# Early operands for the first backward steps of an attention and FFN gradient, and unread TensorE products while its opening waits

## The chip, the cores and the metric

One core of one Trainium2 chip runs the whole program. The metric is the device time of one execution in microseconds (us), of which each kernel was run several times; profiles are of one execution each.

Engine names in the profiles: PE is TensorE's products, PEld its weight loads, DVE VectorE, ACT ScalarE, POOL GpSimd, SP SyncE, whose queue (SPq) issues most transfers (900 of 1066 issues in the trace of the kernel before).

## The reference, cut to what matters

The reference is a transformer block, forward and backward: x of 2048 rows by 448, 16 heads of 28, an FFN of width 1792, in bf16. Outputs are the block's result and the six gradients.

```python
xn = _layernorm(x)
return x + _A_ref(xn, wqkv, wo) + _B_ref(xn, w_gate, w_up, w_down)
# _A_ref: softmax attention, 16 heads;  _B_ref: (silu(x @ w_gate) * (x @ w_up)) @ w_down
_out, _vjp = jax.vjp(_f, A_x, A_wqkv, A_wo, B_w_gate, B_w_up, B_w_down)
return (_out, *_vjp(grad_out))
```

## The kernel before

The kernel runs one fixed order of instructions. An **opening** normalises x, transposes it and makes the first projections. The **forward half** is 256 slots of attention (one key tile, four heads), with the FFN's forward and backward products and most weight gradients filled in between. The **backward half** is 512 steps: `row(k)` computes a score product and a dP product for two heads, `ew(k)` the exponentials (ACT) and ds = dP * e (DVE), and later products use them. Between the halves is the **turn**: the last forward buffers are free only now, and the buffers of the backward half are opened in their place.

`sp_flush()` issues stores that were put off.

```python
def turn_loads():
    nonlocal kq
    sp_flush()                      # four stores of dw_oT are still held here
    ffst.close()
    kq = bwd.enter_context(tc.tile_pool(name="kq", bufs=1, side="right", reuse_waits="tile"))
    SP.dma_start(out=new_k(0, 0)[:], in_=KD_d[0, 0])
    for qc in range(4):
        SP.dma_start(out=new_q(0, qc)[:], in_=QD_d[0, qc])
    SP.dma_start(out=new_k(0, 1)[:], in_=KD_d[0, 1])
```

After the last slot come six last units (PV product, normalisation, output gradient, the softmax correction `mid3`, the projection gradient `dwo_unit`), and the first four backward rows stand between the pieces of the last five:

```python
for u in last[:-5]:
    run(u())
k = n = 0
for u in last[-5:]:
    for _ in u():
        n += 1
        if n in (8, 17, 25, 32):
            row(k)
            ew(k)
            k += 1
K0 = k
sp_flush()                          # stores of odT, the transpose that mid3 issued
fwd.close()
...
for x in pend:                      # DMA transposes of the first ds tiles
    x()
fT = bk.tile([P, 4, 2, 4, P], BF16, name="dsp", bufs=1)
drip(("f",), [(fT[:, a:a + 2], fT_d[:, a:a + 2]) for a in (0, 2)], 10)

def late_dw(c):                     # the last FFN weight gradients, from step 9
    have(("f",))
    ps = ps_g.tile([P, 2, P], FP32, name="genb")
    for t in range(NT):
        PE.matmul(ps[:dn], lhsT=xn_sp[:, t, d0:d0 + dn], rhs=fT[:, t // 4, :, t % 4, :], ...)
```

`late_dw`: its operand `fT` (tile `dsp` in the trace) is stored to HBM at the forward end and loaded back behind the transposes.

The opening, cut:

```python
for t in range(4):
    run(T_unit(xnT, xn_t, t, t % 2 == 0, ps_s if t < 2 else None))   # transposes of x
...
proj(1, 0, True)                    # key, then query projection of the first 512 rows
proj(0, 0)
for c in range(3):
    slot(4 * c); ...
    T(t + 2, t + 3)
    proj(1, c + 1)
```

The softmax here doesn't subtract the row's maximum and nothing guards it: scores larger than these inputs give would overflow.

## Time and profile before

| kernel before, profiled execution | us |
|---|---|
| median of 3 executions (range) | 1441.15 (1439.99 to 1442.68) |
| first exponentials of the forward half | 15.9 |
| exponentials of the last forward slot, 255 | 606.5 |
| first product of backward step 0 | 614.1 |
| first gradient accumulation | 623.0 |
| exponentials of backward step 48 | 689.0 |

Two more views of the kernel before matter in hindsight. The first is the order of time of SP's queue around the turn (start, time of the issue, queue, line, kind, out<-in, count). It was not in the prediction, and most of this document hangs on it:

```profile
607.22 2.12 SPq L206 DMA_DIRECT2D out_dram<-dw_oT  x4
...
619.96 1.29 SPq L200 DMA_TRANSPOSE odT<-od  x1
...
623.67 4.26 SPq L829 DMA_TRANSPOSE dsT<-ds_sb  x3
627.99 1.08 SPq L769 DMA_DIRECT2D dsp<-fT_d  x2
```

Read it as a chain: four stores, then (in the prediction) the loads of keys and queries, then the transpose of od, then three transposes of ds, then the load of dsp. Each stands behind the one ahead of it in one queue. In the kernel before nobody waits for the last one, because TensorE itself comes late.

The second is the granted clock between two stretches of 3.4 us (columns as in the prediction):

```profile
621.30:624.70 3.40, 1.65 (x15) 0.40 (x12) 2.46 (x5) 1.05 (x3) 1.48 (x3) 1.00 0.70 192
624.80:628.20 3.40, 3.40 (x26) 0.61 (x26) 2.85 (x5) 2.14 (x6) 0.53 (x2) 0.50 1.00 189
```

TensorE was busy for 1.65 of 3.40 us and was then given half clock for the next 3.4 us. The stretch behind that, 628.20 to 631.60 us with TensorE busy for 2.58 of 3.40 us, was at full clock and was followed by half clock as well (0.50 from 631.60 to 635.00).

### The profile page before, as it was taken

The numbers are of one execution on the slowest core, as the hardware profiler recorded it, in microseconds if no ns is written. First come the engines' busy times: TensorE is split into PE (matmuls) and PEld (weight loads), VectorE is DVE, ScalarE is ACT, GpSimd is POOL, SyncE is SP. The second block draws the span as 40 slices with busy tenths as digits, with TensorE's granted clock in tenths as the row PEclk, the third lists the DMA queues.
The fourth block names the chain that finished last, engine by engine and source line by source line (L and its number), as shares of the span: only waits on it lengthen the run. The fifth ranks groups of instructions, "written<-read, shape, count | busy, mean of one in ns | idle before, by whom it ended". The sixth has DMA issues, their size and how long they took to land. (4 is left out here: it accounts for less than half of the span.)

```text
span 1440.1 us, 34682 instructions
## 1 busy us (share of the span) xinstructions
PE 1326.3 (92%) x12647; PEld 541.0 (38%) x12708; DVE 1151.8 (80%) x1997; ACT 1261.5 (88%) x2193; POOL 403.6 (28%) x561
## 2 busy tenths in 40 slices
PE   5889999999999999889999999999999999999996
PEld 2333333333333333333333434433443444444343
DVE  6667757666676676578998998888889999989988
ACT  5789988988889999869989989899989999989974
POOL 6464524464334454111112112201111011010006
PEclk9999999999999999989999999999999999999998
DMA  5796956796678586799999999999999999999971
GB/s 154 181 199 165 235 122 160 187 195 164 146 162 192 147 172 145 178 234 226 226 213 217 232 220 188 196 209 229 228 173 194 209 223 230 201 191 203 198 142 60
DMA packets 681179, 271.69 MB, mean 189 GB/s; under 512 B 606424, under 2 KB 655824, under 8 KB 681008
## 3 DMA queue, kind: packets, MB, share of 16 engines
q1 hardware_dynamic: 672576, 255.35, 87.1%
q0 software_dynamic: 7024, 13.82, 4.1%
q8 instruction: 100, 1.64, 0.5%
q14 instruction: 71, 0.58, 0.1%
q10 hardware_dynamic: 1408, 0.30, 0.1%
HBM read 65.09 MB, written 60.36 MB: 87 GB/s over the span
## 5 line engine op out<-in xcount | busy, mean ns | idle before, releaser
L842 DVE TENSOR_TENSOR ds_sb<-db,e_sb 128x512 bf16<-128x512 f32 x1024 | 646.8, 684 | 51.3 <-issue 21.1
L836 ACT ACTIVATE e_sb<-sb 128x512 bf16<-128x512 f32 x1024 | 554.8, 611 | 60.4 <-PE db L820 44.5
L612 ACT ACTIVATE eT<-s_w 128x1024 bf16<-128x1024 f32 x256 | 263.5, 1029 | 46.1 <-PE s_ps L609 43.1
L614 ACT ACTIVATE eT<-s_ps 128x512 bf16<-128x512 f32 x512 | 280.4, 612 | 0.0
L820 PE MATMUL db<-kd,qd 32*128 32x512 bf16 x1024 | 234.4, 384 | 8.2 <-DVE ds_sb L842 7.4
L812 PE MATMUL sb<-kd,qd 32*128 32x512 bf16 x1024 | 210.4, 387 | 5.1 <-DMA qd<-QD_d 3.3
L961 POOL TENSOR_TENSOR dq_acc<-dq_acc,dq_st 128x256 f32<-128x256 f32 x64 | 46.2, 721 | 455.4 <-ACT dq_st L959 455.4
L919 PE MATMUL acc<-ds_sb,qd 128*32 128x512 bf16 x1024 | 161.0, 391 | 0.0
L915 PE MATMUL acc<-e_sb,qd 128*32 128x512 bf16 x1024 | 158.8, 391 | 1.3 <-DVE dw_o L528 1.3
L902 ACT COPY dsT<-db 128x1024 bf16<-128x1024 bf16 x128 | 130.1, 1016 | 14.6 <-PE db L897 13.9
L380 POOL TENSOR_TENSOR nn<-nn,ag 128x512 f32<-128x512 f32 x56 | 71.2, 1271 | 252.2 <-DVE ag L378 243.7
L609 PE MATMUL s_ps<-QQ,KK 32*128 32x512 bf16 x512 | 125.4, 385 | 3.9
L1128 PE MATMUL genb<-wguT,dau_c 128*128 128x448 bf16 x448 | 117.5, 355 | 6.3 <-ACT dq_st L959 3.9
L609 PE MATMUL s_w<-QQ,KK 32*128 32x512 bf16 x512 | 100.3, 387 | 13.1 <-ACT eT L612 10.4
L812 PEld LDWEIGHTS <-qd 32*128 32x128 bf16 x1024 | 48.2, 91 | 149.4 <-issue 140.3
L421 PE MATMUL gen<-xn_t,f_sp 128*128 128x448 bf16 x416 | 91.8, 354 | 2.6 <-DVE nn L395 1.7
L421 PEld LDWEIGHTS <-f_sp 128*128 128x128 bf16 x640 | 55.7, 98 | 75.0 <-issue 31.9
L946 PE MATMUL genb<-dsT,kd 128*32 128x256 bf16 x2048 | 79.5, 275 | 1.9 <-DVE dqT L955 0.6
L897 PE MATMUL db<-ident_bf,ds_sb 128*128 128x128 bf16 x1032 | 79.4, 220 | 1.1 <-DVE ds_sb L842 1.1
L897 PEld LDWEIGHTS <-ds_sb 128*128 128x128 bf16 x1032 | 68.3, 99 | 24.1 <-issue 5.3
L451 PE MATMUL gen<-eT,VS 128*32 128x512 bf16 x1024 | 68.4, 384 | 5.5 <-DVE nn L395 3.3
L381 POOL TENSOR_TENSOR nn<-nn,tt 128x512 f32<-128x512 f32 x56 | 72.0, 1286 | 4.4
(167 smaller groups left out, 1911.0 us busy)
## 6 DMA issues: line engine op xcount, KB each, us to landing
F_d<-hda SPq DMA_DIRECT2D x56, 384.0 KB, 3.1
dau_c<-F_d SPq DMA_DIRECT2D x24, 512.0 KB, 4.4
qd<-QD_d SPq DMA_DIRECT2D x16, 512.0 KB
kd<-KD_d SPq DMA_DIRECT2D x16, 384.0 KB, 4.0
dsT<-ds_sb SPq DMA_TRANSPOSE x383, 4.3
dc<-dqkvT_d SPq DMA_DIRECT2D x12, 384.0 KB, 3.9
h_c<-F_d SPq DMA_DIRECT2D x8, 512.0 KB, 4.4
wT_d<-wT_f SPq DMA_DIRECT2D x14, 256.0 KB, 3.6
```

What stands on the lines that cost most here:

```text
L421: PE.matmul(ps[:, :D], lhsT=fsp[fc][:, t // 4, w, t % 4, :], rhs=rhs[:, t, :], start=(t == 0), stop=(t == NT - 1))
L609: PE.matmul(sp4[hh], lhsT=KK[g][r:r + HP, kt * P:(kt + 1) * P], rhs=QQ[g][r:r + HP, qsl], start=True, stop=True, tile_position=(r, 0))
L612: ACTE.activation(out=e2[0][:], in_=wide[:], func=ACT.Exp, scale=SCALE)
L614: ACTE.activation(out=e2[1][:, j], in_=sp4[2 + j], func=ACT.Exp, scale=SCALE)
L812: PE.matmul(s_ps[:], lhsT=qside[g, qc][r:r + HP, 0, qi * P:(qi + 1) * P], rhs=kside[g, kc][r:r + HP, 0, :], start=True, stop=True, tile_po ...
L820: PE.matmul(d_ps[:], lhsT=qside[g, qc][r:r + HP, 1, qi * P:(qi + 1) * P], rhs=kside[g, kc][r:r + HP, 1, :], start=True, stop=True, tile_po ...
L836: ACTE.activation(out=est[k][:, j], in_=sps.pop((k, j))[:], func=ACT.Exp, scale=SCALE)
L842: DVE.tensor_tensor(out=ds[:, j], in0=dps.pop((k - 1, j))[:], in1=est[k - 1][:, j], op=ALU.mult)
L897: PE.transpose(ps[:, c, :], ds[:, c // 4, (c % 4) * P:(c % 4 + 1) * P], ident_bf[:])
L902: ACTE.copy(out=o, in_=ps[:])
L915: PE.matmul(a[r:r + HP, :], lhsT=sp4[:, 1, r:r + HP], rhs=e[:, j, :], start=first, stop=last, tile_position=(0, r), skip_group_check=True)
L919: PE.matmul(a[r:r + HP, :], lhsT=sp4[:, 0, r:r + HP], rhs=ds[:, j, :], start=first, stop=last, tile_position=(0, r), skip_group_check=True)
```

## The change

Its intent: take the wait for keys and queries out of the turn by loading the first operands 16 slots earlier into a free buffer, start the backward rows sooner, take work off DVE there, and keep TensorE's clock up in the opening with products that nobody reads. The diff, cut to its core:

```diff
+    def warm(ps, n):
+        for _ in range(n):
+            PE.matmul(ps[:], lhsT=ident_bf[:], rhs=ident_bf[:].unsqueeze(1).to_broadcast([P, 4, P]), start=True, stop=True)
 ...
+    warm(genx.tile([P, 512], FP32, name="gen"), 24)          # before the first transposes
-        proj(1, c + 1)
+        proj(1, c + 1, pre=3)                                # three before each of three projections
 ...
     for i in range(16, NS):
         slot(i)
+        if i == NS - 16:
+            sp_flush()
+            first4 = wk.tile([P, S], BF16, name="qk_sp", bufs=1)[:].rearrange("p (a s) -> p a s", a=4)
+            SP.dma_start(out=first4[:, 0:2], in_=KD_d[0, 0, :, 0:2])
+            SP.dma_start(out=first4[:, 2:4], in_=QD_d[0, 0, :, 0:2])
 ...                                                          # in row(k):
+            ks, qs = (first4[:, 0], first4[:, 2]) if k < 4 else (kside[g, kc][:, 0], qside[g, qc][:, 0])
 ...                                                          # in mid3, last call only:
+        (ACTE.copy if end else DVE.tensor_copy)(out=dOl, in_=prod[:])
+        (POOL if end else DVE).tensor_tensor(out=prod[:], in0=prod[:], ...)
+        eng = POOL if (g, qc) == (G - 1, 3) else DVE         # its four small operations
 ...                                                          # in dwo_unit, last call only:
+        (ACTE.copy if g == G - 1 else DVE.tensor_copy)(out=o[:], in_=ps[:, :D])
 ...
-    for u in last[:-5]:
+    for u in last[:-6]:
         run(u())
-    k = n = 0
-    for u in last[-5:]:
+    K0 = 5
+    row(0)
+    ew(0)
+    k = 1
+    for u in last[-6:]:
-            if n in (8, 17, 25, 32):
+            if n in (4, 20, 24, 32):
```

More of the change, by code (lines that the diff above doesn't have):

```diff
@@ L267, in qkv_open, with qkv_unit @@
         VS[g] = wk.tile([P, NT, P], BF16, name="VS")
-    def qkv_unit(g, tq, sc, act=False):
+    def warm(ps, n):
+        for _ in range(n):
+            PE.matmul(ps[:], lhsT=ident_bf[:], rhs=ident_bf[:].unsqueeze(1).to_broadcast([P, 4, P]), start=True, stop=True)
+    def qkv_unit(g, tq, sc, act=False, pre=0):
         if g not in QQ:
@@ L274, in qkv_unit @@
         ps = new_gen([P, 512], FP32, name="gen")
+        warm(ps, pre)
         for c in range(4):
@@ L503, in mid3 @@
         dl = wk.tile([P, 3, 16], FP32, name="dl")
-        DVE.tensor_copy(out=dOl, in_=prod[:])
-        DVE.tensor_tensor(out=prod[:], in0=prod[:], in1=t[:, 0].rearrange("p q (h r) -> p (q h) r", r=HP), op=ALU.mult)
+        end = (g, qc) == (G - 1, 3)
+        (ACTE.copy if end else DVE.tensor_copy)(out=dOl, in_=prod[:])
+        (POOL if end else DVE).tensor_tensor(out=prod[:], in0=prod[:], in1=t[:, 0].rearrange("p q (h r) -> p (q h) r", r=HP), op=ALU.mult)
         yield 0
@@ L508, in mid3 @@
         yield 0
-        DVE.tensor_scalar(out=dl[:, 1, :], in0=dl[:, 0, :], scalar1=-1.0, scalar2=None, op0=ALU.mult)
-        DVE.tensor_copy(out=dOl[:, :, 28], in_=dl[:, 1, :])
-        DVE.tensor_tensor(out=dl[:, 2, :], in0=dl[:, 1, :], in1=dOl[:, :, 28], op=ALU.subtract)
-        DVE.tensor_copy(out=dOl[:, :, 29], in_=dl[:, 2, :])
+        eng = POOL if (g, qc) == (G - 1, 3) else DVE
+        eng.tensor_scalar(out=dl[:, 1, :], in0=dl[:, 0, :], scalar1=-1.0, scalar2=None, op0=ALU.mult)
+        eng.tensor_copy(out=dOl[:, :, 28], in_=dl[:, 1, :])
+        eng.tensor_tensor(out=dl[:, 2, :], in0=dl[:, 1, :], in1=dOl[:, :, 28], op=ALU.subtract)
+        eng.tensor_copy(out=dOl[:, :, 29], in_=dl[:, 2, :])
         tT = wk.tile([P, 2, 4, P], BF16, name="odT")
@@ L527, in dwo_unit @@
         o = wk.tile([P, D], BF16, name="dw_o", bufs=1)
-        DVE.tensor_copy(out=o[:], in_=ps[:, :D])
+        (ACTE.copy if g == G - 1 else DVE.tensor_copy)(out=o[:], in_=ps[:, :D])
         for hh in range(4):
@@ L632, in T, with proj @@
             run(T_unit(xnT, xn_t, t))
-    def proj(tq, sc, act=False):
-        run(qkv_unit(0, tq, sc, act))
+    def proj(tq, sc, act=False, pre=0):
+        run(qkv_unit(0, tq, sc, act, pre))
     def stats4(cc):
@@ L811, in row @@
                 r = HP * (2 * hp + j)
-                PE.matmul(s_ps[:], lhsT=qside[g, qc][r:r + HP, 0, qi * P:(qi + 1) * P],
-                          rhs=kside[g, kc][r:r + HP, 0, :], start=True, stop=True, tile_position=(r, 0))
+                PE.matmul(s_ps[:], lhsT=qs[r:r + HP, qi * P:(qi + 1) * P],
+                          rhs=ks[r:r + HP], start=True, stop=True, tile_position=(r, 0))
                 sps[k, j] = s_ps
@@ L816, in row @@
             g, hp, kc, qc, qi = steps[k - 1]
+            ks, qs = (first4[:, 1], first4[:, 3]) if k <= 4 else (kside[g, kc][:, 1], qside[g, qc][:, 1])
             for j in range(2):
@@ L819, in row @@
                 r = HP * pv(2 * hp + j)
-                PE.matmul(d_ps[:], lhsT=qside[g, qc][r:r + HP, 1, qi * P:(qi + 1) * P],
-                          rhs=kside[g, kc][r:r + HP, 1, :], start=True, stop=True, tile_position=(r, 0))
+                PE.matmul(d_ps[:], lhsT=qs[r:r + HP, qi * P:(qi + 1) * P],
+                          rhs=ks[r:r + HP], start=True, stop=True, tile_position=(r, 0))
                 dps[k - 1, j] = d_ps
@@ L854 @@
     fill.mine = None
-    for u in last[:-5]:
+    for u in last[:-6]:
         run(u())
-    k = n = 0
-    for u in last[-5:]:
+    n = 0
+    K0 = 5
[3 more added lines that the diff above has]
+    for u in last[-6:]:
         for _ in u():
             n += 1
-            if n in (8, 17, 25, 32):
+            if n in (4, 20, 24, 32):
                 row(k)
@@ L864 @@
                 k += 1
-    K0 = k
     sp_flush()
```

## The prediction

> **What bounds the kernel now.** I read the page first, for which engine is full; then the table of busy time by stretch, for where it is not; then the order of time around the two places that the change edits, for what each wait ends on.
>
> The page's busy times and the two rows of slices:
>
> ```profile
> PE 1326.3 (92%) x12647; PEld 541.0 (38%) x12708; DVE 1151.8 (80%) x1997; ACT 1261.5 (88%) x2193; POOL 403.6 (28%) x561
> ...
> PE   5889999999999999889999999999999999999996
> ...
> PEclk9999999999999999989999999999999999999998
> ```
>
> TensorE is busy 90% or more nearly everywhere except in slices 1 to 3 (the opening), slices 18 and 19 (the turn from the forward to the backward half, near 610 us) and the end. In the forward half PE is busy 8.4 to 10 us of each 10 us, ACT 8 to 9.9; in the backward half PE 46 to 49 of each 50 us, with DVE and ACT close behind. So time saved at the two seams should reach the end: both halves are a static order of instructions on a nearly full engine. 512 backward steps in about 777 us are 1.52 us a step, and nothing there waits for a fixed hour.
>
> The turn, in stretches of 2 us (columns: stretch, length, busy time and count of PE, PEld, DVE, ACT, POOL, then granted clock, DMA share, GB/s):
>
> ```profile
> 608.00:610.00 2.00, 1.02 (x4) 0.36 (x4) 0.69 (x1) 0.52 (x2) 0.00 (x0) 1.00 0.48 109
> 610.00:612.00 2.00, 0.84 (x12) 0.65 (x10) 0.95 (x2) 0.00 (x0) 0.00 (x0) 1.00 0.71 191
> 612.00:614.00 2.00, 0.00 (x0) 0.00 (x0) 0.00 (x0) 0.00 (x0) 0.00 (x0) 1.00 1.01 403
> 614.00:616.00 2.00, 1.90 (x15) 1.04 (x16) 0.57 (x1) 1.12 (x3) 0.00 (x0) 0.63 0.98 350
> 616.00:618.00 2.00, 2.00 (x6) 0.60 (x4) 1.93 (x5) 1.05 (x2) 0.00 (x0) 0.51 1.05 420
> ```
>
> No engine works between 612 and 614 us while the DMA moves 403 GB/s, and then the granted clock is half. The order of time names the cause:
>
> ```profile
> 609.44 0.53 SPq L722 DMA_DIRECT2D kd<-KD_d  x1
> ...
> 610.23 0.61 PE L487 MATMUL gen<-woT,dyT 128*128 128x128 bf16 x8
> ...
> 614.10 0.39 PE L812 MATMUL sb<-kd,qd 32*128 32x512 bf16 x2 [3.27 <-DMA qd<-QD_d]
> ...
> 622.98 0.39 PE L915 MATMUL acc<-e_sb,qd 128*32 128x512 bf16 x2 [1.28 <-DVE dw_o L528]
> ```
>
> The first backward score product waits 3.27 us for kd and qd, whose issue (609.44) comes after the last forward buffers are free. From the last forward PV product (ends 608.94) to the first gradient accumulation (622.98) is 14.0 us. The work in it is far less: on PE, by durations and spacings at full clock, transposes 0.6, 16 products of the output gradient about 1.0, four rows about 1.8, 16 products of the projection gradient about 3.0: 6.4 us. On DVE: oacc 0.69, rl and od 0.95, prod 0.69, the last softmax correction 0.43 + 0.69 + 0.61 + 0.75 = 2.48, three pairs of ds products 3.9, dw_o 0.62: 9.3 us.
>
> The opening:
>
> ```profile
> 9.35 1.03 PE L320 MATMUL s_ps<-ident_bf,xn_t 128*128 128x128 bf16 x8 [9.35 <-DMA KK<-in_A_wo_dram]
> ...
> 11.84 2.83 PE L276 MATMUL gen<-xnT,wq_g 128*128 128x512 bf16 x8 [0.61 <-DVE cols L656]
> ...
> 21.70 0.59 PE L276 MATMUL gen<-xnT,wq_g 128*128 128x512 bf16 x1 [0.70 <-DVE xnT L326]
> ```
>
> PE is empty until 9.35 us. Its first projections start 0.43 us apart although the table prints clock 1.00[...]; by 15.8 us four of the same products take 1.04 us. Then the table shows half clock from about 20.6 to 27.4 us and from 41.1 to 44.5 us.
>
> [...]here a 128x512 fp32 product takes 0.69 us on DVE (L505) and 1.27 us on POOL (L380), a factor of 1.8.[...]
>
> **The change part by part.**
>
> 1. Early operands. Two loads of 256 KB each are issued 16 slots before the forward end, near 573 us by slots of 2.2 us, into a buffer whose last user is long done. At the 400 GB/s seen in the turn they cost about 1.3 us of DMA time, where the DMA share is 0.6 to 0.9: hidden. Rows 0 to 3 then need no transfer. Removed: the 3.27 us wait.
>
> 2. Rows moved. Row 0 now stands right behind the last PV product, row 1 behind the four transposes, row 2 behind the 16 output-gradient products, row 3 behind the first of dwo, row 4 behind the ninth. I simulated this with the durations above, starting at 608.94: row 0 at 609.0, its exponentials until 610.6; transposes 609.7 to 610.4; row 1 until 610.8; DVE rl and od until 611.4, ds(0) until 612.7; output gradients 610.9 to 612.1; row 2 until 612.6; prod until 613.4; row 3 waits for a PSUM bank that ds(1) frees at 614.05; eight products of dwo until 615.9; row 4 until 616.4; the rest until 617.9. ACT copies dw_o (about 0.6 us) and the first accumulation starts at 618.7, not 622.98: **4.3 us**. Row 4 and ds(3) are then already done, where they used to follow: row 6 comes at about 620.6 instead of 625.98, so I count **5.4 us** for parts 1 to 3. Row 4 needs the second query block. The first landed at 614.05; 512 KB more at 410 GB/s lands at 615.3, ahead of row 4 at 615.9, by little.
>
> 3. Work off DVE. Copy 0.43, product 0.69, four small operations 0.75 and dw_o 0.62: 2.5 us leave DVE in the turn, against one more ds pair (1.3) before the accumulation. This is what lets DVE (8.1 us of work from 609.0) stay ahead of PE; it is already in the 5.4. The product on POOL takes 1.27 us, while DVE has ds(1) to do.
>
> 4. The clock in the turn. Half clock in 614.3 to 617.7, 624.6 to 628 and 631.5 to 635, by the table. The first is counted in part 2. Without the empty stretch some of the rest may not come, but DVE needs about 1.3 us a step there anyway, against the measured 1.53: estimated gain 0.7 us, between 0 and 2.
>
> 5. 24 unread products at the start. They can begin when the identity is made, at about 1.35 us.[...] The eight projections at full clock save 1.7 us on PE and some 0.7 on the way to the first exponentials, as QQ's copy waits on DVE for statistics until 13.97. But the next projection at 21.70 hangs on the normalisation on POOL (two pieces of 1.9 us from 16.53 to 20.36), which no TensorE speed moves. So most is absorbed.
>
> 6. Three unread products before each of three key projections, where PE waits 0.70, 1.32 and 0.62 us for copies. At full clock they cost 0.65 us and fit; at half clock 1.3, a delay of 0.6 in two of three places.[...] Parts 5 and 6 together: **1.0 us**, between -0.5 and 2.5.
>
> Sum: 5.4 + 0.7 + 1.0 = 7.1; 1441.15 - 7.1 = 1434.05, rounded to 1434.0 us.
>
> **The rivals.** (a) Transfer becomes the wait again: row 4 for the second query block. For it: only 0.6 us of margin. Against it: the transfers land in order, at 410 GB/s. It would give back 1 to 2 us: about 1435.5. (b) DVE or the PSUM banks bound the turn: with three banks each for scores and db, row 3 waits for ds(1), and a POOL product that comes late holds the reduction at the head of DVE's queue. It would give back 1 to 2 us. (c) The backward half hides the gain: the DMA share is over 1 there[...]. Against: the list of waits from 640 to 1395 us has only 3.4 us on a DMA. If so, the gain falls to 2 or 3 us: 1438.5. (d) The clock does more than I think, in both places: 1430. (e) The opening loses, by late transposes and cold fillers: 1436.
>
> **Range and chances.** The before runs spread by 2.7 us[...]. Rivals a, b and e take 1 to 2.5 us each, d gives 4: 1430.0 to 1438.5 for eight in ten. Two per cent are 28.8 us, more than twice the whole turn's 14.0: faster 0.01, same 0.98, slower 0.01.
>
> **What would show it right or wrong.** Right: no engine-free stretch in the turn; the first score products within 0.2 us of the last PV product with no DMA wait; from that product to the first accumulation about 9.8 us instead of 14.0; projections of the opening spaced 216 ns from the first; the first exponentials some 0.7 us earlier, the projection of 21.70 nearly unmoved. Wrong: a wait of row 4 on qd, a wait of DVE's reduction on POOL, half clock still in the opening and longer, or the backward steps at more than 1.52 us each.

The sum was 5.4 + 0.7 + 1.0 = 7.1 us, and so 1434.0 us. Of its terms, the 1.0 us for parts 5 and 6 rested in part on when the unread products would come to full speed and end, and an earlier return of the clock, of which little over 0.5 us was to pass. The savings and costs that remain in parts 5 and 6 (1.7, 0.65 and 1.3 us) come from spacings of starts in the trace of the kernel before: at L276, 427 ns from 12.22 to 13.50 us and again in the half clock from 22.51 us on, 216 ns from 13.86 to 14.29 us; 8 times the difference is 1.7 us, 3 spacings are 0.65 or 1.3 us.

## More of the kernel before

What the backward half reads first is loaded at the turn.

## The result, and the profile after

The changed kernel took 1443.99 us (median of 4, 1441.85 to 1445.77), the kernel before 1440.57 us (median of 4, 1439.41 to 1442.68) in the same rounds. The ratio is 1.0021, with a 95% interval of 1.0002 to 1.0041. All ratios here are the mean time of one kernel's runs over that of the other's of the same rounds, so not quite the ratio of the medians. Instead of 7 us less, it takes about 3 us more. The time lies above the predicted range.

The page of the changed kernel (busy time by engine, then the slices):

```profile
PE 1341.8 (93%) x12741; PEld 545.4 (38%) x12741; DVE 1148.9 (80%) x1990; ACT 1263.1 (88%) x2195; POOL 406.5 (28%) x566
...
PE   7899999999999999989999999999999999999996
...
PEclk9999999999999999989999999999999999999998
```

The opening and the turn have filled up in the slices (7 8 9 for 5 8 8 in front, one 8 instead of two in the middle), and TensorE is busy for 15.5 us more. A fuller row of slices is thus not a shorter time: TensorE was given unread work, and busy time counts longer at half clock (four products of 512 columns take 1.92 us in the opening below, against 1.04 at full clock).

The turn, in stretches of 2 us, of the kernel after:

```profile
612.00:614.00 2.00, 1.98 (x23) 1.00 (x21) 2.00 (x4) 1.76 (x4) 0.00 (x0) 1.00 0.63 184
614.00:616.00 2.00, 1.26 (x8) 0.41 (x5) 1.50 (x3) 1.86 (x4) 0.97 (x1) 1.00 0.74 285
616.00:618.00 2.00, 0.94 (x5) 0.29 (x3) 1.78 (x3) 0.00 (x0) 1.04 (x5) 1.00 0.71 266
618.00:620.00 2.00, 0.78 (x7) 0.37 (x8) 0.25 (x2) 0.35 (x1) 0.14 (x1) 0.98 1.00 387
620.00:622.00 2.00, 2.00 (x6) 0.60 (x5) 1.07 (x2) 0.73 (x2) 0.00 (x0) 0.50 1.23 362
```

The stretch without any engine at work, 612 to 614 us, is gone. A thin one has come instead, from 616 to 620 us, with the DMA at 266 to 387 GB/s and half clock right behind it. It is the old picture, 4 to 6 us later. The order of time names what is waited for:

```profile
609.98 0.39 PE L826 MATMUL sb<-qk_sp 32*128 32x512 bf16 x2
...
619.22 0.39 PE L826 MATMUL sb<-kd,qd 32*128 32x512 bf16 x2 [2.28 <-DMA qd<-QD_d]
...
622.63 0.61 PE L933 MATMUL acc<-e_sb,qd 128*32 128x512 bf16 x2 [0.62 <-ACT dw_o L535]
...
633.75 0.59 PE L899 MATMUL genb<-dsp,xn_t 128*128 128x256 bf16 x2 [1.61 <-DMA dsp<-fT_d]
```

Row 0 reads the early operands (`qk_sp`) and waits for nothing, as predicted. Row 4, the first that needs the second query block, waits 2.28 us for it. Then a product that the prediction never mentions, `late_dw`, waits 1.61 us for dsp. SP's queue of the same kernel shows why:

```profile
608.32 3.20 SPq L206 DMA_DIRECT2D out_dram<-dw_oT  x4
611.63 0.52 SPq L730 DMA_DIRECT2D kd<-KD_d  x1
...
623.71 0.32 SPq L206 DMA_DIRECT2D OT_d<-odT  x1
...
624.63 4.20 SPq L844 DMA_TRANSPOSE dsT<-ds_sb  x3
628.88 1.06 SPq L782 DMA_DIRECT2D dsp<-fT_d  x2
```

Against the last forward slot (607.62 us in this execution, 606.52 in the one before) the load of kd is issued 4.01 us later instead of 2.92, since the four stores ahead of it took 3.20 us to issue instead of 2.12. The load of dsp is issued 21.3 us after that slot, against 21.5 before: that end of the transfer chain hardly moved, while step 5 came 1.9 us sooner after that slot.

The opening of the kernel after:

```profile
1.35 7.40 PE L271 MATMUL gen<-ident_bf 128*128 128x512 bf16 x24 [1.35 <-POOL ident_bf masks.py:199]
...
11.73 1.89 PE L281 MATMUL gen<-xnT,wq_g 128*128 128x512 bf16 x8 [0.61 <-POOL w_f L345]
...
20.78 0.72 PE L325 MATMUL gen<-ident_bf,xn_t 128*128 128x128 bf16 x5 [0.68 <-POOL xn_t L238]
21.29 1.49 PE L271 MATMUL gen<-ident_bf 128*128 128x512 bf16 x3
22.57 1.92 PE L281 MATMUL gen<-xnT,wq_g 128*128 128x512 bf16 x4
```

The unread products start at 1.35 us, the first ten about 427 ns apart and those from 5.56 us on 216 ns apart, and end before the transposes. The eight projections stand 215 to 217 ns apart from the first and take 1.89 us instead of 2.83. The first exponentials come at 14.91 us instead of 15.88. But the transposes ahead of the next projection still wait for the normalisation on POOL, and the three unread products that follow run at half clock (0.50 from 19.18 to 26.01 us). So the projection that stood at 21.70 us now stands at 22.57, itself at half clock (four products in 1.92 us), and the next scores come at 24.41 us instead of 23.50.

### The profile page after: what moved, and what is told of

Same layout as the page of the kernel before. It is cut to its first block, busy times and chain, and to the rows that moved or that the text cites. A ratio compares the mean times of both kernels' runs of the same rounds, so it can differ in the third digit from the quotient of the medians.

```text
span 1440.1 us, 34814 instructions
## 1 busy us (share of the span) xinstructions
PE 1341.8 (93%) x12741; PEld 545.4 (38%) x12741; DVE 1148.9 (80%) x1990; ACT 1263.1 (88%) x2195; POOL 406.5 (28%) x566
## 3 DMA queue, kind: packets, MB, share of 16 engines
q8 instruction: 100, 1.64, 0.5%
## 5 line engine op out<-in xcount | busy, mean ns | idle before, releaser
L616 PE MATMUL s_w<-QQ,KK 32*128 32x512 bf16 x512 | 100.2, 386 | 12.3 <-ACT eT L619 10.5
L616 PEld LDWEIGHTS <-KK 32*128 32x128 bf16 x1024 | 29.2, 91 | 115.1 <-issue 112.0
```

The source lines that it names most:

```text
L616: PE.matmul(sp4[hh], lhsT=KK[g][r:r + HP, kt * P:(kt + 1) * P], rhs=QQ[g][r:r + HP, qsl], start=True, stop=True, tile_position=(r, 0))
```

## The experiments

The experiments follow two theories, which came out of the two traces. **Theory T**: the turn's gain is given back to transfers. The bound there is the order of SP's queue, so that each wait taken away from TensorE reappears at the next transfer in that queue. **Theory O**: the opening costs time on its own, somewhere behind it. The rivals are the clock (chance or not), the work moved to POOL and ACT, and plain spread between executions. The expectations use letters of their own (A, N, C, I, R, S) and say what each means where it first stands.

For the readings, one table is worked out from the traces by starts of exponentials. "255" is the last forward slot; "step k" is a backward step; "half" is the time at half clock between steps 16 and 48.

```
kernel                      255 to step 5   255 to 16   16 to 48   half    255 to 48
before                          18.18         35.13       47.39     3.4      82.52
unchanged again                 18.92         35.10       51.28    13.7      86.38
after                           16.27         35.09       48.47     6.8      83.56
after again                     16.89         37.15       47.28     3.4      84.42
opening alone                   19.33         36.77       45.93     0.0      82.71
turn alone                      14.10         33.83       48.67    10.2      82.51
turn, loads first               13.11         32.40       46.65     0.0      79.05
turn, late_dw later             13.67         28.30       51.15     6.8      79.46
turn, two blocks early          13.10         34.75       47.23     3.4      81.97
turn, all transfers moved       13.11         28.47       53.33    13.7      81.79
turn, loads first, dw later     13.11         27.74       49.91     0.0      77.64
the same, clock kept            13.11         28.07       49.51     0.0      77.59
loads first, DVE's work back    14.48         32.95       48.54     6.8      81.50
```

### Both halves of the change, each alone, and the two kernels again

Four kernels ran on one chip in five rounds: the kernel before once more as if it were a change, the changed kernel again, its opening alone (the two `warm` edits) and its turn alone (everything else).

```diff
# opening alone, against before            # turn alone, against after
+ warm(genx.tile(...), 24)                 - warm(genx.tile(...), 24)
+ proj(1, c + 1, pre=3)                    - proj(1, c + 1, pre=3)  ->  proj(1, c + 1)
```

Unchanged kernel:

> The kernel before, unchanged, as a control. Every theory: ratio 1.000 with an interval of about +-0.001, 1440.6 us. Its second trace against the first shows how far an unchanged program moves by itself: theory A (the change costs something of its own) expects the two traces to agree within about 0.5 us at every forward slot and backward step; theory N (jumps of 0.7 to 2 us in the forward half are chance of the transfers' timing[...]) expects jumps of that size here too.

Changed kernel again:

> The changed kernel, unchanged. If the first result (ratio 1.0021) holds: about 1443.5 us, ratio 1.001 to 1.004. In the trace theory A expects again: row 4 waits some 2 us for the second query block, late_dw waits some 1.6 us for its operand, and half clock for about 14 us between 619 and 640. Theory N expects these to come and go.

Opening alone:

> Only the unread products of the opening, the turn as before. My prediction: ratio 0.9993 (1 us gained). Theory A says the opening gains 1 us to slot 12 as in the first trace and keeps it: 1439.6 us. Rival: the opening loses what it gained in the forward half[...]: 1440 to 1443 us.

Turn alone:

> Only the turn's part (early operands, rows moved, work off vector engine), no unread products. Theory A: the turn gives back what it gains by the wait of row 4 and by half clock, so 1440 to 1442 us, and the trace shows the wait of row 4. My prediction said 1435. If this is at 1443.5 and the opening only at 1440, the turn is the one that costs.

Measured, median (range) of 6 runs, and ratio with interval against the 11 runs of before in these rounds (mean 1442.43): unchanged 1441.02 (1435.35 to 1444.70), 0.9984 [0.9958, 1.0010]; after again 1444.48 (1442.80 to 1447.00), 1.0015 [0.9995, 1.0035]; opening alone 1443.30, 1.0003 [0.9982, 1.0024]; turn alone 1441.09, 0.9988 [0.9963, 1.0012].

What follows. The kernel before itself ranges from 1437.09 to 1447.79 us within this one session; the 2.7 us that the prediction took for its spread were three runs. The loss of the changed kernel repeats. By means in the same rounds, the turn alone is worth -1.5 us (standard error 1.7), and adding the opening to it costs +4.0 us (1444.92 less 1440.97; standard error 1.5). The opening alone, against the kernel before, costs less: +0.7 us (1443.13 less 1442.43; standard error 1.2). So these rounds show no gain of the opening, but not how much it costs. Neither half shows what was predicted of it (-6.1 and -1.0 us). In the table the turn alone gains 4.1 us by step 5, has 1.3 left at step 16, and nothing at step 48.

### Where the turn's gain goes

Four edits of the turn alone, three rounds. Loads first: the loads of keys and queries are issued ahead of the four held stores.

```diff
     def turn_loads():
-        sp_flush()
+        hold = late[:]
+        late.clear()
 ...
         SP.dma_start(out=new_k(0, 1)[:], in_=KD_d[0, 1])
+        late.extend(hold)
+        sp_flush()
```

> The turn's part alone, with the turn's loads of kd and qd issued ahead of the last four small stores instead of behind them. Theory T (the turn is paced by the in-order queue of transfers: 2.8 MB of loads, then the stores that wait for the last transposes, then dsT, then the operand of late_dw): issue of kd 2 to 3 us earlier, the wait of row 4 (1.5, 2.3 and 3.0 us so far) under 0.5 us, and the stretch from the last forward exponential to step 16 shorter by 1.5 to 2.5 us than the 33.8 of the turn alone. Rival C (half clock alone paces it): the stretch stays within 1 us although the wait goes.

late_dw later: the transfers stay as they are, and `late_dw` begins with step 17 instead of step 9.

```diff
-        if 9 <= k < NB and cur is None:
+        if 17 <= k < NB and cur is None:
-            if 9 <= k < NB:
+            if 17 <= k < NB:
```

> The turn's part alone, with the first filler work (late_dw, which needs the late operand) from step 17 instead of step 9. Theory T: no wait on that operand, and the stretch to step 16 shorter by about 5 us (wait 3.0, and its own products of some 2 us moved behind): 28 to 30 us; how much of it is left at the end tells whether the work moved is free: at most 3 us. Rival C: half clock still costs, the stretch is 31 us or more.

Two blocks early: the second query block is also loaded 16 slots ahead, so that rows 4 to 7 wait for nothing either.

```diff
+            next2 = wk.tile([P, 4, 3, P], BF16, name="wqT_st", bufs=1)[:]...
+            SP.dma_start(out=next2, in_=QD_d[0, 1, :, 0:2])
-            ks, qs = (first4[:, 0], first4[:, 2]) if k < 4 else (kside...
+            ks, qs = (first4[:, 0], first4[:, 2] if k < 4 else next2[:, 0]) if k < 8 else (kside...
```

> The turn's part alone, with the second query block's operands early as well, so that rows 4 to 7 too need no load of the turn. Theory T: the wait of row 4 goes, but the first gradient accumulation still needs the whole first block and late_dw its operand: the wait there grows by about what is won (3.0 to 4 or 5 us) and step 16 moves by under 1 us. My prediction's reasoning (each wait removed is time won): step 16 comes 1.5 us earlier.

All transfers moved: loads first, two blocks early, and the load of fT ahead of the last stores and of the ds transposes.

```diff
     drip(("f",), [(fT[:, a:a + 2], fT_d[:, a:a + 2]) for a in (0, 2)], 10)
+    have(("f",))        # issue the load of fT now
+    for x in pend:      # and only then the transposes of ds and the stores of odT
+        x()
+    sp_flush()
 ...                # cut: the edits of the two kernels above, and another buffer for the transpose of od
```

> The turn's part with loads first, two early blocks, and the operand of late_dw issued ahead of the last stores and of the dsT transposes. Theory T: none of the three waits is over 0.5 us, the stretch from the last forward exponential to step 16 is 29 to 31 us against 35.1 of the kernel before, and the time some 4 us below the kernel before: ratio 0.997. Rival C: 33 us or more.

Measured (before: 7 runs, mean 1442.21): loads first 1443.29, 1.0004 [0.9978, 1.0031]; late_dw later 1440.27, 0.9994 [0.9967, 1.0022]; two blocks 1442.78, 1.0005 [0.9978, 1.0033]; all 1440.22, 0.9978 [0.9947, 1.0008]. Four runs each could not separate these kernels by their times, so the traces have to speak.

They do. Taking away the wait for the second query block, in three of the four, brings step 5 to the same 13.10 or 13.11 us. In the kernel with two blocks the wait did not vanish; it moved, and grew. Its TensorE, at `late_dw`:

```profile
632.52 0.58 PE L900 MATMUL genb<-dsp,xn_t 128*128 128x256 bf16 x2 [5.43 <-DMA dsp<-fT_d]
```

The turn alone waits 2.99 us there, and this kernel 5.43, after it had saved 1.52 us at row 4. By step 16 it is at 34.75 us, later than the turn alone. The two kernels that take this wait away, one by moving the reader (late_dw later) and one by moving the transfer (all), are at 28.30 and 28.47 us at step 16, 6.7 to 6.8 us ahead of the kernel before. With late_dw later a part of this is only put off, since the products of `late_dw` then come behind step 16; with all transfers moved they stay where they were, and start at 629.46 us without a wait. This is theory T as it stood, with a number on each link.

The gain is not fully carried on: from step 16 to 48 the kernel with all edits has 13.7 us at half clock and is the slowest of all there (53.33), so that little is left at step 48 (81.79 against 82.52). It is no verdict on the edit: the unchanged kernel, run again, shows the same 13.7 us and 51.28. In the table the half clock between these steps adds up to 0.0, 3.4, 6.8, 10.2 or 13.7 us, and it lies differently from trace to trace: at 672.6 to 676.0 us in the kernel before, at 667.7 to 671.1 and 674.5 to 678.0 us in the changed one.

### Both transfer edits, with and without a kept clock; DVE's work put back; added instructions

Loads first and late_dw later together, on the turn alone, with five rounds, as the candidate:

> The turn's part alone, with the turn's loads issued first and late_dw from step 17: no wait on a transfer in the turn should be left. Theory T: last forward exponential to step 16 in 27 to 28.5 us (35.1 before), to step 48 in 77 to 80 us[...] (82.5 and 86.4 before); time 1438 us, ratio 0.997. If the time is the same as before within 1 us although the turn is 4 us shorter, the gain is given back later than step 48.

The same with unread products in steps 5 to 35, to test whether the clock holds back the rest:

```diff
+        if 5 <= k < 36 and cur is None and m in (0, 3):
+            warm(ps_g.tile([P, 512], FP32, name="genb"), 2)
```

> As the run before it, with two unread products at two of four steps from 5 to 35 where no filler runs, to keep the clock. Theory C (half clock between steps 5 and 48 costs about 0.4 us for each us of it): no half clock between steps 5 and 48, and step 48 comes 1 to 3 us earlier than without these products; time 1437 us. Rival: the stretch is bound by vector engine at 1.3 us a step and the products only add work: step 48 no earlier, or later by up to 2 us.

The 0.4 us in it is an estimate; the table's first two lines give such a figure (51.28 less 47.39 us, for 13.7 less 3.4 us of half clock).

"Loads first" with the softmax correction and the copy of dw_o back on DVE (one look, state unknown):

```diff
-        (ACTE.copy if end else DVE.tensor_copy)(out=dOl, in_=prod[:])
+        DVE.tensor_copy(out=dOl, in_=prod[:])
-        eng = POOL if (g, qc) == (G - 1, 3) else DVE
+        eng = DVE
 ...                                     # cut: the product and the copy of dw_o, likewise
```

> The turn's part with loads first, but the last softmax correction and the copy of dw_o back on vector engine as in the kernel before. My prediction's part 3 says that the 2.5 us taken off vector engine are what keeps it ahead: then step 5 comes 1 to 2.5 us later than the 13.1 us with loads first alone. Rival: tensor engine has the slack, under 0.5 us.

And, for theory O, the kernel before with 33 unread products of one column, as many instructions as the opening adds with hardly any work:

```diff
+    one = genx.tile([P, 512], FP32, name="gen")
+    for _ in range(33):
+        PE.matmul(one[:, 0:1], lhsT=ident_bf[:], rhs=ident_bf[:, 0:1], start=True, stop=True)
```

> The kernel before with 33 unread products of one column at the start: as many added instructions on tensor engine as the opening of the change has, but almost no work. In the three traces with the unread products the stretch from slot 192 to 204 takes 26.95 to 27.26 us against 25.6 to 26.2 in the seven without[...] and slots 240 to 252 take 26.6 against 27.1 to 27.4. Theory I (the added instructions shift the fetches, whatever they compute): 26.9 or more and 26.6 here too, and the fetch some 4 us earlier than in the kernel before, against slot 200. Rival (the opening's other timing does it): 25.6 and 27.3.

Measured (before: 11 runs, median 1445.44): the candidate 1438.45 (1436.11 to 1442.17), **0.9955 [0.9927, 0.9984]**; clock kept 1439.52, 0.9969 [0.9938, 1.0000]; DVE's work back 1442.06 (one run); one column 1448.95 (1447.44 to 1452.46), 1.0029 [0.9995, 1.0064].

The candidate's queue and TensorE:

```profile
606.33 0.38 SPq L730 DMA_DIRECT2D kd<-KD_d  x1
...
609.61 2.56 SPq L206 DMA_DIRECT2D out_dram<-dw_oT  x4
```

```profile
614.88 0.39 PE L828 MATMUL sb<-kd,qd 32*128 32x512 bf16 x2
...
617.92 0.39 PE L935 MATMUL acc<-e_sb,qd 128*32 128x512 bf16 x2 [0.62 <-ACT dw_o L535]
```

The load of kd now goes out 3.3 us ahead of the stores, row 4 waits for no transfer, and the first accumulation stands 12.29 us after slot 255. At step 48 this kernel is 4.9 us ahead of the kernel before (77.64 against 82.52). Here the gain of the turn does arrive.

The kept clock is a miss, as an idea: no half clock from step 5 to 48, yet step 48 is at 77.59 us against 77.64. The candidate itself had only one half-clock stretch in the turn. So its clock was no bound in that execution; what more half clock would have cost, this pair cannot show.

Putting the work back on DVE makes step 5 later by 1.37 us (14.48 against 13.11). In these lines, the same dP product first in "loads first", then with the work put back:

```profile
618.47 0.37 PE L837 MATMUL db<-qk_sp 32*128 32x512 bf16 x1 [0.23 <-DVE ds_sb L859]
```

```profile
621.20 0.37 PE L837 MATMUL db<-qk_sp 32*128 32x512 bf16 x1 [1.56 <-DVE ds_sb L859]
```

So moving that work was worth its while for the turn itself: a wait of 1.56 us on DVE instead of 0.23. By step 16 only 0.55 us of it is left: `late_dw` waits for dsp in both, 1.87 us instead of 2.74.

The one-column kernel is the surprise. Its added work is 1.04 us at a time when TensorE has nothing else to do, and its runs average 1449.45 against 1445.03 us (standard error of the difference 1.7). In its trace slots 192 to 204 take 27.05 us. They take 26.95 to 27.26 in all traces with the opening, and 25.53 to 26.21 in all traces without added products, where most other groups of slots repeat to 0.01 us. So it is the added instructions that cost there, not the work of 512-column products.

What differs at slot 199 is a transfer that no line of the kernel issues. The page counts the fetches of instructions as a queue of their own (`q8 instruction: 100, 1.64, 0.5%` in the kernel before: 100 packets, 1.64 MB, 16 KB each). One packet came 2.4 to 3.0 us after slot 199's exponentials in the traces without products added at the start, and 2.1 to 2.4 us before them in those with (at 482.2 us in the kernel before, at 477.6 us in the kernel after). (A second instruction queue on the page, q14, has its nearest packet 0.3 to 0.8 us ahead of slot 199 in all traces, so it does not make the difference.) In that stretch a store of dw_o is under way, whose buffer DVE wants next. The kernel before, then the kernel after:

```profile
479.65 0.62 DVE L528 CAST dw_o<-gen 128x448 bf16<-128x448 f32 x1 [3.43 <-PE s_ps L609]
```

```profile
481.40 0.62 DVE L535 CAST dw_o<-gen 128x448 bf16<-128x448 f32 x1 [5.06 <-DMA out_dram<-dw_o]
```

In the first DVE waits for TensorE's next scores, in the second for the store. Not every kernel without added products looks like the first line: some wait for the store too, for 3.5 to 4.0 us. What separates all traces is when that store lands: 2.9 to 3.5 us after its issue where the packet comes behind, 4.0 to 4.3 us where it comes ahead. This gives theory O a sharper form, **theory F**: 33 products are 66 instructions, a product and its weight load each (the pages of the kernel before and after count 12708 and 12741 weight loads), and by this theory they shift at which instruction of the program each packet is fetched.

### The whole change with the turn mended, against the turn alone

Five rounds on one chip: the whole change with loads first and late_dw later, and the candidate.

> The whole change, opening included, with loads first and late_dw from step 17. If the opening is worth nothing and its added instructions cost what the table of slots shows (slots 192 to 204 longer by 1.3 us, 240 to 252 shorter by 0.7), this is 0 to 2 us above the same kernel without the opening, which runs beside it. If the opening gains the 1 us that I predicted, it is 1 us below. In the trace: slots 192 to 204 in 26.9 to 27.3 us, the turn to step 16 in 27.7 to 28.5 us.

> Turn's part with loads first and late_dw from step 17, again, as the partner of the run with the opening and to see whether the ratio of 0.9955 holds: 0.995 to 0.998, turn to step 16 in 27.7 to 28.5 us.

Measured (before: 11 runs, mean 1440.98): the whole change mended 1444.95, 1.0027 [0.9999, 1.0055]; the candidate 1437.92 (1433.99 to 1440.37), 0.9980 [0.9955, 1.0005]. By means the opening costs 7.2 us here (standard error 2.0), more than the 0 to 2 us expected. In both, step 5 is at 13.11 us and step 16 at 27.01 and 28.36, so the turn's gain is there in both. The whole change thus has a mended turn and still loses, by its opening.

### The test of the fetch position

How many instructions a packet stands for can be estimated from the pages: the kernel before has 12647 products and 12708 weight loads beside 100 packets, 254 for each packet, the kernel after 12741 and 12741 beside 100, 255. That this queue carries TensorE's instructions alone is assumed in it and not shown. 128 added products with their weight loads are 256 instructions, by this estimate one packet more, and all later packets would stand at the same instructions again. So theory F says that 128 added products cost less than 33. Four kernels in five rounds: the candidate with 33 one-column products, with 128, the whole change mended with 95 one-column products ahead of its 33 (128 in all), and the candidate as it is.

```diff
# on the candidate                        # on the whole change, mended
+    for _ in range(33):   # or 128       +    for _ in range(95):
+        PE.matmul(one[:, 0:1], ...)      +        PE.matmul(one[:, 0:1], ...)
                                               warm(one, 24)
```

> The turn's changes with loads first and the late product later, no opening, and 33 unread one-column products at the start (66 instructions of TensorE). Theory F (the opening costs by moving where the 16 KB packets of instructions are fetched): slots 192 to 204 take 27.0 to 27.3 us instead of 25.7, a packet comes some 2.2 us ahead of slot 199, and the time is 1 to 5 us above the same kernel with no added products. Rival R (the cost comes from the opening's 512-column products, their clock and the earlier start): no difference beyond 1.5 us. Rival S (chance between builds): no order to be told.

> The same with 128 one-column products: 256 instructions[...]. Theory F: slots 192 to 204 back at 25.7 us, the packet behind slot 199's exponentials again (2.6 us), time within 2 us of the kernel with none. If added instructions cost in proportion: worse than with 33. Rival R: as with none.

> The whole change with loads first and the late product later, and 95 one-column products ahead of the 24, so that 128 products are added in all[...]. Theory F: slots 192 to 204 at 25.7 us, and the time within 2.5 us of the kernel without the opening, where the two stood 7 us apart before. Rival R: 27 us no longer, yet still 4 to 7 us slower than without the opening, the cost then lying in the opening's products or in the early start.

> The comparison for the other three on the same chip: the turn's changes with loads first and the late product later, nothing added at the start. Both theories: slots 192 to 204 25.7 us, the first accumulation 12.3 us after the last forward exponentials, step 48 at 77 to 78 us, and some 3 to 6 us faster than the kernel before.

Measured (before: 11 runs, median 1440.52), with the place of the nearest packet against slot 199's exponentials, from the traces:

```
kernel                  median us   mean us   slots 192-204   packet at slot 199
candidate + 33           1444.44    1443.30       26.84             -2.55
candidate + 128          1436.88    1438.86       26.21             +2.66
whole, mended + 95       1437.41    1438.49       25.76             +2.62
candidate                1438.93    1439.70       25.77             +2.65
```

The ratios to before are 1.0019 [0.9989, 1.0048], 0.9991 [0.9959, 1.0023], 0.9985 [0.9957, 1.0014] and 0.9994 [0.9969, 1.0019]. The page's line of the instruction queue (packets, MB, share) in the kernels with 33 and with 128:

```profile
q8 instruction: 100, 1.64, 0.5%
```

```profile
q8 instruction: 101, 1.65, 0.5%
```

With 128 there is exactly one packet more, and the packet at slot 199 is back where it was. The kernel with 33 is 4.3 us slower than the mean of the other three (1443.30 against 1439.02; standard error about 1.7) and 3.6 us slower than the plain candidate (standard error 1.7), and the whole change, which stood 7.2 us behind the candidate, stands level with it once it is padded. The test came out as theory F said. That the cost came from the 512-column products themselves does not: the padded kernel has them all. One thing is not tested by it: its 24 products ran later, behind the 95, and its first exponentials came at 16.69 us, so the early start of the opening is not in it.

Where the cost lies can be read from all traces with a timeline, grouped by the place of the packet: six with it ahead of slot 199, twelve with it behind (without the kernel with kept clock and the one with unknown state).

```
mean us                     packet behind (12)    ahead (6)    difference
slot 36 to slot 255              500.24             502.65        +2.4
step 48 to step 208              245.50             247.88        +2.4
step 208 to step 511             455.28             455.57        +0.3
step 511 to the end               49.23              48.51        -0.7
```

Together that is +4.4 us, much like the times; the standard errors of the four differences are 0.6, 1.0, 0.4 and 0.3. In single stretches only slots 192 to 204 (+1.3) and their answer in slots 240 to 252 (26.6 instead of 27.3) are clean, and together they are only 0.6 of the 4.4 us; the rest overlaps between single executions. The turn is a second clean place. In the six traces with the packet ahead, another packet comes 0.5 to 1.0 us after slot 255's exponentials, next to the issue of the turn's first transfers; in the other twelve none comes there within 5 us. Where the four stores go first, their issue takes 2.8 to 3.25 us with that packet and 2.1 without, so that the load of kd goes out at 3.6 to 4.05 us instead of 2.92 after slot 255.

That a packet delays the transfers beside it fits these two places; it is a reading, and the rest of the 4.4 us is not traced to single packets. The runs show that the number of added instructions does it, and the place of the packets with it.

The candidate's three sessions: 18 runs with a mean of 1438.68 us, against 1442.53 for the 33 runs of before in the same sessions, 3.8 us or 0.27% less. Its three ratios lie below 1, one of them with its whole interval; the two of the changed kernel lie above 1. So it beats both kernels, the kernel before by little.

## Why the prediction was wrong, point by point

**Part 1, early operands: right as far as it went.** Rows 0 to 3 wait for no transfer, and the two early loads disturb nothing that can be seen.

**Part 2, rows moved: the computing was right, its path was not the bound.** The simulated turn put the first accumulation 12.2 us after slot 255 (618.7 less 606.52); with the transfers out of the way it is 12.29 us. The gain at step 6 was put at 5.4 us; the same kernels show 6.0 (14.08 us from slot 255 to step 6, against 20.10). The failing step is "lands at 615.3, ahead of row 4 at 615.9, by little", 8.8 and 9.4 us after slot 255. Row 4 was ready at 9.3 us, as computed, but the block came at 10.4 to 12.3 us: row 4 waited 2.28, 3.01, 1.52 and 1.09 us in the four traces with the new rows and that order. Two terms were too small. The main one is the transfer. From the issue of kd to row 4 the prediction allows 5.9 us, with 410 GB/s at the end; the four traces show 7.5 to 8.7 us, at 265 to 303 GB/s on average. The turn alone issues its loads as early as the kernel before and waits all the same:

```profile
608.75 0.52 SPq L729 DMA_DIRECT2D kd<-KD_d  x1
...
616.66 0.39 PE L825 MATMUL sb<-kd,qd 32*128 32x512 bf16 x2 [1.52 <-DMA qd<-QD_d]
```

"The transfers land in order" does not fit either: 2.0 to 2.6 MB moved in that time, by those rates, where kd and the two query blocks have 1.4 MB. Why the transfer took longer stays open. The second term is the issue, 4.01 and 3.63 us after slot 255 in the two traces of the changed kernel instead of 2.92; the opening alone (3.61) and one column (4.05) show the same, so it came with the added instructions and not with the turn. Rival (a) named this wait and about its size, yet I gave it little weight.

**The step that was missing altogether.** The sum followed TensorE and DVE and stopped at row 6; no rival followed SP's queue past the loads. `late_dw` reads dsp, whose load stands behind the last stores and the ds transposes. It waited 1.61 and 2.62 us in the two traces of the changed kernel, and 5.43 us in the kernel with two blocks, where row 4 no longer waited. The sentence "nothing there waits for a fixed hour" is what failed. Rival (c), that the backward half hides the gain, came true, but the argument against it, only 3.4 us of DMA waits from 640 us on, looked past the stretch from 622 to 640 and at a kernel whose TensorE was late enough not to wait.

**Part 3, DVE's relief: right.** It is worth 1.37 us at step 5. DVE's reduction did wait for POOL's product, as rival (b) feared, 0.72 us in the changed kernel and 0.73 in the candidate; the candidate's first accumulation came at the simulated time all the same.

**Part 4, the clock: not shown.** Nothing of the 0.7 us can be seen. Half clock in the turn up to step 16 was 10.2 and 13.7 us in the two traces of the kernel before, 13.7 and 10.2 in the two of the changed one. So it differs as much between two executions of one kernel as between the kernels. Keeping the clock by force brought nothing, beside a candidate that had only 3.4 us of half clock to lose.

**Parts 5 and 6, the opening: the near part right, the sum wrong in sign.** The unread products began when predicted (1.35 us), the first exponentials came about 1 us earlier (0.7 predicted), and by the next projection, behind the normalisation on POOL and its own unread products, it was gone: 22.57 us against 21.70. The four traces with the opening as changed reach slot 36 at 105.2 to 107.2 us, and those without it at 104.3 to 109.6. What the sum lacked is a cost of the instructions as such. A gain of 1.0 us was predicted; losses of 0.7, 4.0 and 7.2 us (standard errors 1.2, 1.5 and 2.0) were measured in three comparisons, and padded to 128 products the opening costs nothing that can be seen (1.2 us less than without it, standard error 1.6).

**The range.** It was built on 2.7 us, the spread of three runs. The 55 runs of the kernel before beside the others, over several chips, range over 18.6 us (1436.08 to 1454.66), and those of one session with 11 of them over 10.3 to 15.6 us. Three runs do not give a spread, and an expected gain of 7 us in 1441 needs rounds on one chip to be seen at all. (One reading was off by one, and nothing rests on it: the turn stands in slices 17 and 18 of the page's row, not 18 and 19.)

In sum, -6.1 us for the turn became -1.5, and -1.0 us for the opening became between +0.7 and +4.0 in the rounds that ran both halves. In those rounds the changed kernel stood 2.5 us above the kernel before, and 3.1 us in the first rounds (means 1443.90 and 1440.81).

## What to carry to other kernels

When a wait on a transfer is taken away, follow the queue that carries it, transfer by transfer, as far as the next reader: here the wait moved from row 0 to row 4 and on to a weight gradient ten steps later, and two edits of order (loads ahead of stores, a reader moved back) let the turn's gain arrive, 4.9 to 5.4 us by step 48 in its three traces and 3.8 us in the time, where the change as it stood gained nothing. Then give a candidate that adds TensorE instructions a sister padded until its later packets stand where they did (here 128 products, 101 packets on the page's line where 33 left 100) before its idea is judged, since 66 instructions with next to no work moved this kernel by about 4 us in both tests (4.4 and 4.3 us). And take the spread from many rounds, not from three runs.
